# Split products for the rows' scales, a last output tile in two halves, and two rests in the second transform stage

## The chip, the core and the metric

The kernel runs on one core of one Trainium2 chip. The metric is the device time of one execution in microseconds. A core has five engines with a queue each: TensorE (PE; its weight loads are shown as PEld), VectorE (DVE), ScalarE (ACT), GpSimd (POOL) and SyncE (SP), which here only issues transfers. An engine works off its queue in order; a transfer (DMA) is issued from a queue and lands later.

## The reference

Two branches share a layer norm of q (here x); everything is fp32, S = 2048 rows, D = 576 channels, DFF = 4608.

```python
k_shift = sum(k_pad[:, t:t+S, :] * shift_k[:, ks-1-t] for t in range(4))
kv = k_shift * v
y = irfft(rfft(kv padded to 2S) * rfft(ssm_k padded to 2S))[:S] + kv * ssm_D     # per channel
...
xn = layernorm(x)
out = x + xn * y + relu(xn @ w1) @ w2
```

## The kernel before

**The FFN branch is the frame.** Tokens lie in 16 tiles of 128 rows, in two halves of 8; a half has two blocks b of 4 tiles (512 tokens). DFF is cut into 18 chunks of 256, so there are 36 "quads" g (18 for each half). A quad makes the hidden values of both blocks, `psh = w1 . x`, and the second product `pso = hidden . w2` of the quad before is made between its pieces, tile by tile. fp32 precision comes from fp32r products of split operands: each value is a rounded part (`hh`, `x[:, 0]`) plus a rest (`ll`, `x[:, 1]`), three products for one. From the fourth quad on (`PLAIN = 3`) seven products of sums replace eight. The order on PE in such a quad is: product 00, units 0 and 1, product 01, rest hl, unit 2, product s2, unit 3, product s1, unit 4, product s3, rest hl, product s4, units 5 and 6, rest hl of the second block, unit 7, product 11, rest hl. A "unit" is the 12 products of one token tile with w2 (`mm2`); DVE then adds the tile into `acc` (L752). Two results are put together on DVE (L686 `u2`, L693 `p5`), and ACT writes the negative of one PSUM bank into another (L688), which PE waits for before it adds the third `rest hl` of the quad: `y` is read by L688 and then written on by PE.

```python
nc.vector.tensor_tensor(u2, x, u2, OP.add)             # L686
x = bank(g, 0, "4")
nc.scalar.activation(x, y, AF.Copy, scale=-1.0)        # L688
hidden(g, 0, 1, u2); unit(5); unit(6)
rest(y, g, b1, 1)                                      # PE's next write of y
```

**The convolution runs in the gaps.** The generator `conv`/`stages` writes a long convolution by DFTs as a stream of steps. `tick` gives it turns: each piece of FFN work adds its cost to a clock, and steps are drawn from the stream as long as the stream's own count is not ahead. A step may yield a cost, `"wide"` (the next step needs a PSUM slot of a unit), or a negative number: a set rest, for so much FFN cost no step is drawn, and the count restarts at 0. `PAUSE` is 16000; a product of 512 columns costs 512.

**The second stage** (L987 to L1098) multiplies spectra. There are 18 rounds n. `product_of(n)` makes the spectrum of the input on PE (psf, two banks), the filter's spectrum of round n+1 (psg, a borrowed slot; ACT copies it out at L1024, SP shuffles its partitions by four DMAs at L1029), then four multiplications on DVE (L1051), which need the psf banks and the shuffled filter; four DMAs (L1056) shuffle the product. `join(n)` (L1063, DVE) needs those. `way_back(n)` does the inverse of two joined rounds. `first_spectrum` stands ahead of round 0. The output stage follows (groups of two token tiles: PE at L1157, DVE gates L1129 and adds L1137, z loaded by SP at L1114).

**The start.** The first three quads use rows that are centred but not yet scaled. The scales 1/std are spread along the free axis by a product: `diagonal` puts them on the diagonal of 128x128 blocks, `scales` multiplies by `ones` (L327), and ACT copies `row` out.

**Order.** A tracking layer sets waits between engines, and a scheduler with its own time model sets the order on each queue from the written order and `tc.issue_after`.

Of the kernel before, what the change touches and what calls it, by code (L numbers as in the profile page):

```python
# [10 lines left out]
F32 = mybir.dt.float32  # L11
F32R = mybir.dt.float32r
AF = mybir.ActivationFunctionType
OP = mybir.AluOpType
# [3 lines left out]
P = 128  # L18
# [5 lines left out]
NH = D // 2  # L24
# [6 lines left out]
BT = T // NB  # L31
# [17 lines left out]
PAUSE = 16000  # L49
# [11 lines left out]
W_FB, W_FS, W_FK, W_FX, W_FMK, W_FMX, W_FMB, W_FO = 2.8, 4.1, 2.5, 1.75, 4.0, 3.6, 2.9, 3.9  # L61
# [38 lines left out]
def h3_ffn_kernel(ctx: ExitStack, tc, x, k, v, shift_k, ssm_k, ssm_D, w1, w2, fwd, inv, mid, out):  # L100
    nc = tc.nc
    x = x[0].rearrange("(p u t) d -> u p t d", u=U, t=T)
    k = k[0].rearrange("(p u t) d -> u p t d", u=U, t=T)
    v = v[0].rearrange("(p u t) d -> u p t d", u=U, t=T)
    out = out[0].rearrange("(p u t) d -> u p t d", u=U, t=T)

    const = ctx.enter_context(tc.tile_pool(name="const", bufs=1))
# [8 lines left out]
    ident = const.tile([P, P], F32, name="ident")  # L116
    make_identity(nc, ident)
    mv = const.tile([P, T, 2], F32, name="mv")
    rstd = const.tile([P, T], F32, name="rstd")
# [20 lines left out]
    def fft_psum():  # L140
        return ps_f.tile([P, 512], F32, tag="f", name="psf")
# [9 lines left out]
    def two(t):  # L151

        return t.rearrange("p (h n) -> p h n", h=2)


    acc = {}

    def halves(u):

        return slice(u * A1, (u + 1) * A1), slice((1 - u) * A1, (2 - u) * A1)  # L160

    def move(tile_, rows, t, store=False, queues=(nc.sync, nc.sync)):
        for u in range(U):
            a, b = tile_[halves(u)[0]], rows[u, :, t]
            queues[u].dma_start(*((b, a) if store else (a, b)))
# [3 lines left out]
    def load_acc(t, **queues):  # L169
        pair = xp.tile([P, 2, D], F32, tag=f"acc{t % HT}", name=f"acc{t}")  # L170
        move(pair, x, slice(t, t + 2), **queues)
        pairs[t] = pair
        acc[t], acc[t + 1] = pair[:, 0, :], pair[:, 1, :]
# [7 lines left out]
    def inv_std(t0, n):  # L181

        q = xp.tile([P, 3, 2 * BT], F32, tag="q", name=f"q{t0}", bufs=2)[:, :, :n]
        va, h0, qu = q[:, 0, :], q[:, 1, :], q[:, 2, :]
        nc.vector.tensor_scalar(va, mv[:, t0:t0 + n, 1], EPS, None, op0=OP.add)
        nc.scalar.activation(h0, va, AF.Sqrt, scale=0.25)
        nc.vector.reciprocal(qu, h0)
        nc.vector.tensor_tensor(qu, va, qu, OP.mult)
        nc.vector.scalar_tensor_tensor(qu, qu, 0.25, h0, op0=OP.mult, op1=OP.add)
        return nc.vector.reciprocal(rstd[:, t0:t0 + n], qu)  # L190
# [6 lines left out]
    done = {}  # L197
# [116 lines left out]

    def diagonal(pool, b):
        diag = pool.tile([P, 2, D], F32, tag="xn", name=f"diag{b}", bufs=4)
        diag = diag[:, 0, :BT * P].rearrange("p (i n) -> p i n", i=BT)
        for i in range(BT):
            nc.vector.tensor_scalar(diag[:, i, :], ident, rstd[:, b * BT + i:b * BT + i + 1],
                                    None, op0=OP.mult)  # L320
        return diag

    def scales(pool, b, diag):

        ps = fft_psum()
        with tc.issue_after(done["pe"].ins):
            done["pe"] = nc.tensor.matmul(ps, ones, diag.rearrange("p i n -> p (i n)"),  # L327
                                          start=True, stop=True)
        row[b] = pool.tile([P, 512], F32, tag=f"row{b}", name=f"row{b}")
        nc.scalar.activation(row[b], ps, AF.Copy)  # L330

# [234 lines left out]
    def matmuls(ps, seq, start):  # L566


        for n, (a, m) in enumerate(seq):
            with tc.issue_after(done["pe"].ins) if "pe" in done and not n else nullcontext():  # L570
                last = nc.tensor.matmul(ps, a, m, start=start and n == 0, stop=n == len(seq) - 1,  # L571
                                        skip_group_check=True)
        done["pe"] = last
# [134 lines left out]
    def token(g, b, i):  # L708
        return (g // NQ) * HT + b * BT + i
# [16 lines left out]
    def mm2(g, b, i):  # L726
        t = token(g, b, i)
        end = g == QUADS - 1
        if end:
            while t not in added:  # L730
                next(stream)
        cols = slice(i * P, (i + 1) * P)
        ps, slot["closed"] = open_ps.pop((g, t))
        unwritten.discard(slot["closed"])
        slot["units"] += 1
        for h in range(2):
            dc = slice(h * NH, (h + 1) * NH)
            seq = []
            for f in range(FT):
                hh, ll = hid[g, b, f]  # L740
                for a, m in ((hh, 0), (hh, 1), (ll, 0)):
                    seq.append((a[:, cols], w2s[g, f][:, m, dc]))
            matmuls(ps[:, h, :NH], seq, t not in seeded)
        if t in seeded:
            done["act"] = nc.scalar.activation(two(acc[t]), ps[:, :, :NH], AF.Copy)
            seeded.remove(t)
        elif g < PLAIN:
            done["acc"] = nc.vector.scalar_tensor_tensor(two(acc[t]), ps[:, :, :NH],
                                                         rstd[:, t:t + 1], two(acc[t]),
                                                         op0=OP.mult, op1=OP.add)  # L750
        else:
            done["acc"] = nc.vector.tensor_tensor(two(acc[t]), ps[:, :, :NH], two(acc[t]), OP.add)  # L752
        tick(W_UNIT, False)
        if g == NQ - 1 and t % 2:
            nc.sync.dma_start(fin[t // 2], pairs[t - 1])
            load_acc(t - 1 + HT)
        if end:
            if b == 1 and i >= BT - 2:
                move(acc[t], out, t, store=True, queues=(nc.sync, nc.scalar))
            elif t % 2:  # L760
                move(pairs[t - 1], out, slice(t - 1, t + 1), store=True)
# [39 lines left out]
    def stages(view, views):  # L801
# [280 lines left out]
            load(zx, n, "x")  # L1082
        yield -PAUSE
        first_spectrum()
        yield W_FMK
        for n in range(NCH // 2 + 1):
            if n in pairs_n:
                yield "wide"
            if n:
                join(n - 1)  # L1090
            if n in pairs_n:
                product_of(n)
            yield W_FMK / 2 + W_FMX
            if n and n % 2 == 0:
                yield "wide"
                way_back(n - 2)
            if n:
                yield W_FMK / 2 + W_FMB  # L1098
# [112 lines left out]
    load_acc(BT + 2)  # L1211
    for j in range(FT):
        load_w2(0, j)
    ones = const.tile([P, P], F32, name="ones")
    nc.vector.memset(ones, 1.0)
    table = const.tile([P, 1], F32, name="table")
    nc.vector.memset(table, 1.0)
    nc.scalar.activation(table, table, AF.Sqrt)
# [8 lines left out]
    with tc.tile_pool(name="fa", bufs=1) as fa:  # L1227
        block_xT(fa, 0, ("00", "01"), (None, None), block_rows(fa, 0))
        xn = block_rows(fa, 1)
        classical(0, 0, 0, 1)  # L1230
        classical(0, 0, 1, 2)
        block_xT(fa, 1, ("10", "11"), ("s4", None), xn)
        load_w1(1)
        with tc.issue_after(done["low"].ins):
            inv_std(0, 2 * BT)
        with tc.issue_after(done["centred"].ins):
            for j in range(FT):
                split_w2(0, j)
                load_w2(1, j)
        classical(0, 1, 0, 0)  # L1240
        split_a(1)
        classical(0, 1, 1, 0)
        split_r(1)
        split_b(1)
        split_d(1)
        load_w1(2)
        diag = {b: diagonal(fa, b) for b in (1, 0)}

        def unit(g, b, i, upto):
            open_unit(g, b, i)  # L1250
            mm2(g, b, i)
            post(1, upto)

        for g in range(1, PLAIN):
            now = "00" if g < PLAIN - 1 else "10"
            for f in range(FT):
                for i in range(2):
                    unit(g - 1, 0, 2 * f + i, "00")
                if g == 1:
                    scales(fa, 1 - f, diag[1 - f])  # L1260
                if g == f == 1:
                    posts["at"] = second_half_of_start(fa)
                classical(g, 0, f, 0, 3, now if f else "00")
            for j in range(FT):
                split_w2(g, j)
                load_w2(g + 1, j)
            for i in range(BT):
                unit(g - 1, 1, i, now)
            classical(g, 1, 0, 0, 3, now)
            split_a(g + 1)  # L1270
            if g + 1 == PLAIN:
                sums(g + 1)
            split_r(g + 1)
            classical(g, 1, 1, 0, 3, None if g == PLAIN - 1 else now)
            split_b(g + 1)
            split_d(g + 1)
            load_w1(g + 2)
        quad(PLAIN, [(PLAIN - 1, b, i) for b in range(2) for i in range(BT)])
        post(99)
# [36 lines left out]
```

## Time and profile before

| what | value |
|---|---|
| median of 3 runs | 1026.66 us (1026.35 to 1027.32) |
| profiled execution, its own time | 1028.02 us |
| its span, first to last instruction | 1026.2 us |
| PE busy / DVE / ACT / POOL | 1011.8 / 709.2 / 429.7 / 486.8 us |
| mean granted TensorE clock | 0.998 |

Rows of the timeline read: start, duration, engine (a q behind its name is its queue, issuing), line, operation, out<-in, engine tile if any, shape, and in brackets how long the engine was idle just before and what ended it. Rows that follow each other on an engine and are alike are merged (x4). Rows of the waits read: engine, line, what it waited for: total, times, longest. Rows of the windows: each engine's busy time with its instructions, then the granted clock, the share of the DMA engines and GB/s.

### The profile page before, as it was taken

The page shows a single profiled execution, that of the slowest core. Times are in us where ns is not written, and L with a number is a line of the kernel's source. Part 1 is how long each engine was busy: PE and PEld are TensorE (multiplying, and loading weights), DVE is VectorE, ACT ScalarE, POOL GpSimd, SP SyncE. Part 2 cuts the span into 40 slices and gives each one's busy share as a digit, 9 for nine tenths or more (in the row PEclk, how much of TensorE's full clock was granted, in tenths as well). Part 3 has the DMA queues.
Part 4 walks back from the last instruction along what each step waited for, and adds up shares of the span by engine and source line. Part 5 has one row for each costly group of instructions (what it writes and reads, how often), then busy time and mean ns, then how long its engine had stood idle before and what let it go on. Part 6 is the DMA issues. An engine that isn't in the chain of part 4 may idle for free.

```text
span 1026.2 us, 17380 instructions
## 1 busy us (share of the span) xinstructions
PE 1011.8 (99%) x6506; PEld 845.9 (82%) x6506; DVE 709.2 (69%) x1075; ACT 429.7 (42%) x761; POOL 486.8 (47%) x532
## 2 busy tenths in 40 slices
PE   9999999999999999999999999989999999999997
PEld 5898999998988889888878889867767777788777
DVE  6787677776465567779787889456656676656765
ACT  7244334443344444444434444444535355332220
POOL 4335446659544557555545455414423344344450
PEclk9999999999999999999999999999999999999999
DMA  7114467558245565369943433677778887857784
GB/s 177 48 44 117 116 173 168 181 175 200 73 134 174 179 196 146 112 208 370 277 139 125 137 97 115 205 222 222 228 227 245 236 264 238 225 189 238 207 256 116
DMA packets 92249, 184.70 MB, mean 180 GB/s; under 512 B 32082, under 2 KB 44500, under 8 KB 91268
## 3 DMA queue, kind: packets, MB, share of 16 engines
q1 hardware_dynamic: 73588, 123.47, 39.8%
q0 software_dynamic: 18256, 59.22, 20.0%
q10 hardware_dynamic: 320, 0.88, 0.3%
q8 instruction: 51, 0.84, 0.3%
q14 instruction: 34, 0.28, 0.1%
HBM read 119.04 MB, written 45.61 MB: 160 GB/s over the span
## 4 chain that ended last, share of the span: by engine, by line
PE 87%; DVE 4%; POOL 2%; DMA 2%; issue 2%; ACT 1%; SPq 1%; DVEq 0%; POOLq 0%; ACTq 0%
PE pso L571 40%; PE psh L571 34%; PE psf L765 5%; PE psg L765 4%; PE psh_c L571 3%; DMA area<-area 1%; POOL area L812 1%; PE psw L1223 1%; DMA r<-in_w 1%; DVE area L944 1%; DVE area L1051 1%; DVE area L945 0%; SPq L1029 0%; DVE sums L527 0%; DVE x L295 0%
## 5 line engine op out<-in xcount | busy, mean ns | idle before, releaser
L571 PE MATMUL pso<-w,hh 128*128 128x288 f32 x2304 | 468.4, 297 | 0.0
L571 PEld LDWEIGHTS pso<-w,hh 128*128 128x128 f32 x2304 | 378.6, 188 | 34.8 <-issue 15.6
L571 PE MATMUL pso<-w,ll 128*128 128x288 f32 x1152 | 340.0, 295 | 0.0
L752 DVE TENSOR_TENSOR acc<-pso,acc 128x576 f32<-128x576 f32 x243 | 183.0, 754 | 157.4 <-PE pso L571 157.1
L571 PEld LDWEIGHTS pso<-w,ll 128*128 128x128 f32 x1152 | 216.8, 188 | 0.0
L515 POOL TENSOR_TENSOR wb<-sums,wb 128x512 fp32r<-128x512 f32 x33 | 51.2, 1552 | 236.1 <-ACT wb L514 208.5
L515 POOL TENSOR_TENSOR w<-r,w 128x576 fp32r<-128x576 f32 x72 | 107.8, 1505 | 106.9 <-ACT w L514 105.8
L571 PE MATMUL psh<-x,wa 128*128 128x512 f32 x396 | 102.9, 395 | 0.5 <-POOL wa L515 0.3
L571 PE MATMUL psh<-xs,wb 128*128 128x512 f32 x396 | 102.0, 393 | 0.0
L571 PE MATMUL psh<-hl,wr 128*128 128x512 f32 x264 | 85.9, 407 | 6.3 <-ACT psh L688 6.3
L571 PEld LDWEIGHTS psh<-x,wa 128*128 128x128 f32 x396 | 72.3, 188 | 16.1 <-POOL wa L515 0.8
L571 PEld LDWEIGHTS psh<-xs,wb 128*128 128x128 f32 x396 | 70.8, 188 | 11.4
L515 POOL TENSOR_TENSOR wa<-r,wa 128x512 fp32r<-128x512 f32 x36 | 53.7, 1490 | 52.8 <-ACT wa L514 52.8
L595 DVE SCALAR_TENSOR_TENSOR ll<-psh,hh 128x512 fp32r<-128x512 f32 x66 | 45.2, 685 | 40.9 <-ACT hh L593 40.7
L688 ACT ACTIVATE psh<-psh 128x512 f32<-128x512 f32 x33 | 19.2, 582 | 128.2 <-DVE u L686 128.2
L571 PEld LDWEIGHTS psh<-hl,wr 128*128 128x128 f32 x264 | 46.0, 188 | 27.1 <-issue 13.2
L765 PE MATMUL psf<-area 64*64 64x512 f32 (+10 forms) x592 | 61.1, 473 | 0.0
L593 ACT ACTIVATE hh<-psh 128x512 fp32r<-128x512 f32 x66 | 39.4, 597 | 49.7 <-PE psh L571 49.0
L765 PE MATMUL psg<-area 64*64 64x512 f32 (+10 forms) x568 | 55.3, 453 | 0.0
L593 ACT ACTIVATE hh<-p 128x512 fp32r<-128x512 f32 x33 | 20.9, 632 | 79.1 <-DVE p L693 43.2
L1024 ACT ACTIVATE area<-psg 128x1024 f32<-128x1024 f32 x34 | 33.2, 1025 | 48.7 <-PE psg L765 48.1
L1051 DVE TENSOR_TENSOR area<-psf,area 128x512 f32<-128x512 f32 x72 | 44.7, 681 | 9.4 <-DMA area<-area 6.7
(140 smaller groups left out, 1525.1 us busy)
## 6 DMA issues: line engine op xcount, KB each, us to landing
r<-in_w POOLq DMA_DIRECT2D x70, 288.0 KB, 3.4
area<-area SPq DMA_DIRECT2D x144, 128.0 KB, 3.8
r<-in_w POOLq DMA_DIRECT2D x35, 512.0 KB, 5.1
zk<-area SPq DMA_DIRECT2D x64, 144.0 KB, 2.3
area<-zk SPq DMA_DIRECT2D x18, 512.0 KB, 4.5
area<-zx SPq DMA_DIRECT2D x18, 512.0 KB, 3.9
zy<-area SPq DMA_DIRECT2D x18, 512.0 KB, 4.8
area<-zy SPq DMA_DIRECT2D x32, 288.0 KB, 5.4
```

The lines of the kernel that those rows point to most:

```text
L515: nc.gpsimd.tensor_tensor(w[:, 1, :n], src, w[:, 0, :n], OP.subtract)
L571: last = nc.tensor.matmul(ps, a, m, start=start and n == 0, stop=n == len(seq) - 1, skip_group_check=True)
L593: done["act"] = nc.scalar.activation(hh, ps, AF.Relu)
L595: nc.vector.scalar_tensor_tensor(ll, ps, 0.0, hh, op0=OP.max, op1=OP.subtract)
L688: nc.scalar.activation(x, y, AF.Copy, scale=-1.0)
L752: done["acc"] = nc.vector.tensor_tensor(two(acc[t]), ps[:, :, :NH], two(acc[t]), OP.add)
L765: done["pe"] = nc.tensor.matmul(ps, a, m, start=start, stop=stop, skip_group_check=True)
L812: nc.gpsimd.dma_start(kt[halves(h)[0], d:d + KD, :], src)
L944: nc.vector.tensor_tensor(e, win[t - n], sk[:, n, :], OP.mult)
L1024: nc.scalar.activation(dst, src, AF.Copy)
L1051: nc.vector.tensor_tensor(filt[c][:, k, :], banks[k], filt[c][:, k, :], OP.mult)
L1223: last = nc.tensor.matmul(idle[0], warm[:, :P], warm, start=True, stop=True)
```

## The change

Four places. (1) The scales are split into a rounded part and a rest (`inverse`, made by a copy and a subtraction on DVE), the diagonals are made by multiplications with broadcast operands, two for each block, and each of the two fp32 products becomes two fp32r products. (2) The last unit of the last quad adds and stores each 288-column half by itself, on the SP and ACT queues. (3) After the first spectrum the stream rests for 8000 instead of yielding a cost of 4.0. (4) After round 0 it rests for 12000 instead of yielding 5.6.

```diff
+        diag = diag[:, :, :BT * P].rearrange("p k (i n) -> p k i n", i=BT).bitcast(F32R)
+        for k in range(2):
+            part = inverse[:, k, b * BT:(b + 1) * BT].unsqueeze(2).to_broadcast([P, BT, P])
+            nc.vector.tensor_tensor(diag[:, k], ident.unsqueeze(1).to_broadcast([P, BT, P]),
+                                    part, OP.mult)
...
-            done["pe"] = nc.tensor.matmul(ps, ones, diag.rearrange("p i n -> p (i n)"),
-                                          start=True, stop=True)
+            for k in range(2):
+                done["pe"] = nc.tensor.matmul(ps, ones, diag[:, k].rearrange("p i n -> p (i n)"),
+                                              start=k == 0, stop=k == 1)
...
             matmuls(ps[:, h, :NH], seq, t not in seeded)
+            if end and b == 1 and i == BT - 1:
+                done["acc"] = nc.vector.tensor_tensor(acc[t][:, dc], ps[:, h, :NH], acc[t][:, dc],
+                                                      OP.add)
+                for u, queue in enumerate((nc.sync, nc.scalar)):
+                    queue.dma_start(out[u, :, t, dc], acc[t][halves(u)[0], dc])
+        if end and b == 1 and i == BT - 1:
+            return
...
         first_spectrum()
-        yield W_FMK
+        yield -PAUSE / 2
...
-            yield W_FMK / 2 + W_FMX
+            yield W_FMK / 2 + W_FMX if n else -0.75 * PAUSE
...
-    ones = const.tile([P, P], F32, name="ones")
-    nc.vector.memset(ones, 1.0)
+    ones = const.tile([P, P], F32R, name="ones")
+    nc.vector.tensor_scalar(ones, ident, 0.0, 1.0, op0=OP.mult, op1=OP.add)
+    inverse = const.tile([P, 2, 2 * BT], F32R, name="inverse")
...
             inv_std(0, 2 * BT)
+            nc.vector.tensor_copy(inverse[:, 0], rstd[:, :2 * BT])
+            nc.vector.tensor_tensor(inverse[:, 1], rstd[:, :2 * BT], inverse[:, 0], OP.subtract)
```

**Where the order changes: DVE at rounds 0 and 1.** The rows are DVE's queue in quad 25 between the adds of units 4 and 7. `sign` marks `join(0)`, `psf` the multiplications of round 1, `u2_25` is L686. Before:

```order
L752 TENSOR_TENSOR acc12_5207<-pso24_12_7027,acc12_5207 128x576
L527 TENSOR_TENSOR sums26_7128<-r1_26_6898 128x256 x2
L527 TENSOR_TENSOR sums26_7128<-sums26_7128,r1_26_6898 128x256
L1063 SCALAR_TENSOR_TENSOR area_1173<-area_1173,sign_85 128x1024
L527 TENSOR_TENSOR sums26_7128<-sums26_7128,r1_26_6898 128x256
L1051 TENSOR_TENSOR area_1173<-psf_7101,area_1173 128x512
L1051 TENSOR_TENSOR area_1173<-psf_7102,area_1173 128x512
L1051 TENSOR_TENSOR area_1173<-psf_7101,area_1173 128x512
L1051 TENSOR_TENSOR area_1173<-psf_7102,area_1173 128x512
L686 TENSOR_TENSOR u2_25_7025<-psh25_5_7041,u2_25_7025 128x512
```

And now (L686 has become L688, L1051 L1060, L1063 L1072):

```order
L529 TENSOR_TENSOR sums26_7101<-sums26_7101,r1_26_6899 128x256 x2
L688 TENSOR_TENSOR u2_25_7026<-psh25_5_7042,u2_25_7026 128x512
L761 TENSOR_TENSOR acc12_5208<-pso24_13_7081,acc12_5208 128x576
L597 SCALAR_TENSOR_TENSOR ll25_0_1_7123<-u2_25_7026,hh25_0_1_7122 128x512
L761 TENSOR_TENSOR acc14_5290<-pso24_14_7126,acc14_5290 128x576
L1072 SCALAR_TENSOR_TENSOR area_1174<-area_1174,sign_85 128x1024
L695 TENSOR_TENSOR p5_25_7076<-psh25_2_6934,p5_25_7076 128x512
L1060 TENSOR_TENSOR area_1174<-psf_7157,area_1174 128x512 x2
L1060 TENSOR_TENSOR area_1174<-psf_7158,area_1174 128x512 x2
```

`u2_25` now stands ahead of round 1's join and multiplications. On PE round 1 moves from behind product s3 of quad 25 to behind the third rest hl; round 0 keeps its place.

**DVE at rounds 7 and 8.** All later rounds shift too. PE's places in quads 25 to 29, with s1, s2, s3, x01 for the products, hl for the second rest, hl3 for the third: before, round 5 behind s2 and round 6 behind hl in quad 27, round 7 behind x01 and round 8 behind s1 in quad 28, round 9 behind product 11 of 28, round 10 behind s2 of 29; now round 5 behind s1 and 6 behind hl3 in 27, 7 behind s2 and 8 behind s3 in 28, 9 behind x01 and 10 behind s1 in 29, with the fifth way back behind hl of 29. DVE's queue in quad 28 had no round between the add of unit 4 (`pso27_12`) and `u2_28`; now it has:

```order
L761 TENSOR_TENSOR acc12_5208<-pso27_12_7971,acc12_5208 128x576
L1072 SCALAR_TENSOR_TENSOR area_1174<-area_1174,sign_85 128x1024
L529 TENSOR_TENSOR sums29_8045<-r1_29_7818 128x256 x2
L1060 TENSOR_TENSOR area_1174<-psf_8018,area_1174 128x512 x2
L529 TENSOR_TENSOR sums29_8045<-sums29_8045,r1_29_7818 128x256
L1060 TENSOR_TENSOR area_1174<-psf_8019,area_1174 128x512 x2
L529 TENSOR_TENSOR sums29_8045<-sums29_8045,r1_29_7818 128x256
L688 TENSOR_TENSOR u2_28_7969<-psh28_5_7985,u2_28_7969 128x512
```

Round 8's join and multiplications stand ahead of `u2_28`, as round 1's and round 6's stood ahead of `u2_25` and `u2_27` before.

**PE at the last unit.** The rows are PE's queue for the last tile, with the semaphores that a row waits for (DVE_49 counts DVE's instructions):

```order
L573 MATMUL pso35_15_10354<-w235_10068,hh35_1_0_10243 128x288 [waits DVE_49]
L573 MATMUL pso35_15_10354<-w235_10068,hh35_1_0_10243 128x288
L573 MATMUL pso35_15_10354<-w235_10068,ll35_1_0_10244 128x288
L573 MATMUL pso35_15_10354<-w235_10146,hh35_1_1_10212 128x288 x2
L573 MATMUL pso35_15_10354<-w235_10146,ll35_1_1_10213 128x288
L573 MATMUL pso35_15_10354<-w235_10068,hh35_1_0_10243 128x288 [waits DVE_49]
L573 MATMUL pso35_15_10354<-w235_10068,hh35_1_0_10243 128x288
```

Before, only the first of the twelve products waited; now the seventh, the first of the second half, waits for DVE as well. Its count in the built program is that of the first half's add: both halves lie in one PSUM tile.

**DVE at the scales**, behind the last `ll` of the first quad. Before, the eight `diag` rows stood ahead of the first `acc0`; now the first `acc0` stands between the copy and the subtraction:

```order
L1246 CAST inverse_127<-rstd_84 128x8
L757 SCALAR_TENSOR_TENSOR acc0_104<-pso0_0_436,rstd_84,acc0_104 128x576
L1247 TENSOR_TENSOR inverse_127<-rstd_84,inverse_127 128x8
L320 TENSOR_TENSOR diag1_430<-ident_78,inverse_127 128x512
L320 TENSOR_TENSOR diag0_433<-ident_78,inverse_127 128x512
L320 TENSOR_TENSOR diag1_430<-ident_78,inverse_127 128x512
L320 TENSOR_TENSOR diag0_433<-ident_78,inverse_127 128x512
```

Block 1's second diagonal, which the first of the two scale products needs, is DVE's sixth row from here.

More of the change, by code (lines that the diff above doesn't have):

```diff
@@ L316, in diagonal @@
         diag = pool.tile([P, 2, D], F32, tag="xn", name=f"diag{b}", bufs=4)
[L317 to L320, printed above, removed]
+        diag = diag[:, :, :BT * P].rearrange("p k (i n) -> p k i n", i=BT).bitcast(F32R)
[3 more added lines that the diff above has]
+                                    part, OP.mult)
         return diag
@@ L757, in mm2 @@
         if end:
-            if b == 1 and i >= BT - 2:
+            if b == 1 and i == BT - 2:
                 move(acc[t], out, t, store=True, queues=(nc.sync, nc.scalar))
```

## Prediction

> **What bounds the kernel.** I read the page's busy shares first, then the waits of PE, then windows of 20 us, then the timeline where the windows show PE short.
>
> ```profile
> PE 1011.8 (99%) x6506; PEld 845.9 (82%) x6506; DVE 709.2 (69%) x1075; ACT 429.7 (42%) x761; POOL 486.8 (47%) x532
> PE psh L571 <- ACT psh L688: 6.3, 3, 2.7
> 500.00:520.00 20.00, 18.89 (x117) 16.96 (x115) 17.71 (x22) 6.50 (x11) 11.13 (x11) 1.00 0.83 228
> 520.00:540.00 20.00, 19.16 (x125) 16.56 (x126) 16.12 (x22) 9.68 (x18) 9.63 (x11) 0.91 0.48 139
> 680.00:700.00 20.00, 17.31 (x107) 14.15 (x103) 13.08 (x21) 6.57 (x11) 5.70 (x7) 1.00 0.71 194
> 740.00:760.00 20.00, 18.33 (x120) 14.12 (x120) 13.07 (x22) 7.51 (x12) 4.23 (x5) 1.00 0.81 217
> ```
>
> PE is the bound. Time can come only from its few gaps, from work taken off it, or from the ends. Three waits for L688 make 6.3 us; one lies near 520, in the first stage, where the order is unchanged. The other two lie in the second stage. The first:
>
> ```profile
> 674.32 1.09 PE L765 MATMUL psf<-area 64*64 64x512 f32 x8
> 677.51 2.48 DVE L1051 TENSOR_TENSOR area<-psf,area 128x512 f32<-128x512 f32 x4 [3.71 <-DMA area<-area]
> 679.37 1.80 PE L765 MATMUL psf<-area 64*64 64x512 f32 x8
> 681.93 2.45 SPq L1029 DMA_DIRECT2D area<-area  x4
> 683.73 1.29 DVE L1063 SCALAR_TENSOR_TENSOR area<-area,sign 128x1024 f32<-128x1024 f32 x1 [2.07 <-DMA area<-area]
> 686.20 2.48 DVE L1051 TENSOR_TENSOR area<-psf,area 128x512 f32<-128x512 f32 x4 [0.84 <-DMA area<-area]
> 688.60 0.68 DVE L686 TENSOR_TENSOR u<-psh,u 128x512 f32<-128x512 f32 x1
> 689.95 0.74 PE L571 MATMUL psh<-hl,wr 128*128 128x512 f32 x2 [2.69 <-ACT psh L688]
> ```
>
> Round 0 starts at 674.32, round 1 already at 679.37. Its multiplications L1051 need the filter that the L1029 transfers shuffle, queued on SP behind round 0's. They land at 686.20. DVE stands still for them, L686 is queued behind, ACT's L688 behind that, and PE misses 2.69 us. Round 1's psf also took 1.80 instead of 1.09: the banks were still being read by round 0's L1051.
>
> ```profile
> 738.13 1.09 PE L765 MATMUL psf<-area 64*64 64x512 f32 x8
> 739.39 2.47 DVE L1051 TENSOR_TENSOR area<-psf,area 128x512 f32<-128x512 f32 x4
> 746.62 1.09 PE L765 MATMUL psf<-area 64*64 64x512 f32 x8
> 748.90 1.28 DVE L1063 SCALAR_TENSOR_TENSOR area<-area,sign 128x1024 f32<-128x1024 f32 x1 [2.59 <-DMA area<-area]
> 750.93 1.29 DVE L1051 TENSOR_TENSOR area<-psf,area 128x512 f32<-128x512 f32 x2 [0.41 <-DMA area<-area]
> 753.67 0.68 DVE L686 TENSOR_TENSOR u<-psh,u 128x512 f32<-128x512 f32 x1
> 755.02 0.73 PE L571 MATMUL psh<-hl,wr 128*128 128x512 f32 x2 [1.67 <-ACT psh L688]
> ```
>
> The second is the same chain between rounds 5 and 6, 8.5 us apart. From a round's start to the next filter's landing it was 11.9 us (674.32 to 686.20) and 12.8 us (738.13 to 750.93). A third pair, rounds 7 and 8, has 11.4 us (767.16 to 778.60):
>
> ```profile
> 767.16 1.09 PE L765 MATMUL psf<-area 64*64 64x512 f32 x8
> 775.66 1.09 PE L765 MATMUL psf<-area 64*64 64x512 f32 x8
> 778.60 2.48 DVE L1051 TENSOR_TENSOR area<-psf,area 128x512 f32<-128x512 f32 x4 [1.19 <-DMA area<-area]
> ```
>
> There no PE time was lost: round 8 stood behind product s1, with unit 4, s3, hl and s4 still ahead of L686. So what decides is the distance of a round to the one before, and whether L1051 stands ahead of `u2` on DVE.
>
> **The rests.** By the order, round 1 goes behind the third rest hl, where `u2_25` and `p5_25` are ahead of its multiplications: the wait of 2.69 us goes. So do the 0.71 us of psf (1.80 - 1.09), since round 0's L1051 ends at 679.99 and round 1 now starts about 685. Late next there is the add of unit 7, behind L1051 until about 688.7; its slot is not needed again before two products and a unit have passed, over 4 us: nothing. Round 6 also goes behind the third hl: 1.67 us go. The rest of 8000 alone moves no row of PE: round 0 keeps its place, as it had to wait for a free slot anyhow.
>
> SP issues the same DMAs, each later with its round, and only loads of zk change places with shuffles. ACT's copies L1024 fall behind `hh` rows and POOL's loads of inv and stores of out behind weight splits; both queues are idle over half the span (42% and 47% above), which hides that. The last output group moves from behind s3 to behind the third hl of quad 35, some 5 us; its stores have the last eight units (8 x 1.59, half of the row 37.32 below) to land in.
>
> But all rounds shift, and one pair becomes tight. Round 8 is now behind s3, round 7 behind s2 of the same quad: between their starts lie 8.0 us, the 8.5 of rounds 5 and 6 without the two products of hl. Round 5 stood in exactly this place behind s2, with a way back ahead of it at the same distance, so I take its 12.8 us to the landing. L686 then follows 3.1 us later (750.93 to 753.67 is 2.74, plus one more of the `sums`, about 0.4, that now stands between). PE resumes 1.35 us after L686's start (753.67 to 755.02). That is 12.8 + 3.1 + 1.35 = 17.25 us after round 7's start; PE would arrive without a wait at 15.22 (755.02 - 1.67 - 738.13; the same work). A new wait of 2.0 us. With a landing after 11.4 us it is 0.6; one that never holds DVE makes it 0. The ends are 0 and 2.4. I take 1.9, by the row of the same place.
>
> Round 10, 8.5 us behind round 9, is the second tight pair; its L1051 end before `u2_29` is due, but the fifth way back, a round, a unit, s3 and hl later (5.5 us), needs its psf banks. With a landing after 11.4 us the first bank is free at 4.8 (2.9 and three of the four L1051), with 12.8 at 6.2: 0 to 0.7 us; I take 0, since the row of this pair (7 and 8 above) is 11.4. Sum of the rests: -2.69 - 0.71 - 1.67 + 1.9 = -3.2 us.
>
> **The scales.**
>
> ```profile
> 29.56 0.17 DVE L189 SCALAR_TENSOR_TENSOR q<-q 128x8 f32<-128x8 f32 x1
> 30.77 3.03 DVE L319 TENSOR_SCALAR diag<-ident,rstd 128x128 f32<-128x128 f32 x8
> 41.27 1.89 DVE L340 TENSOR_TENSOR xf<-xf,row 128x512 f32<-128x512 f32 x3
> 46.93 0.98 DVE L340 TENSOR_TENSOR xf<-xf,row 128x512 f32<-128x512 f32 x1
> 32.97 1.12 PE L327 MATMUL psf<-diag,ones 128*128 128x512 f32 x2 [0.29 <-DVE diag L319]
> 34.10 3.22 PE psh_c L571 x14
> 37.32 3.18 PE pso L571 x24
> 40.50 0.86 PE psf L327 x2
> ```
>
> On the chain (the last three rows) the second fp32 product costs 0.86 us; an fp32r product of the same shape costs 0.23 (3.22/14), two of them 0.46. The second scales save 0.40. The first wait for DVE: from 30.77 a copy (0.17 as the 128x8 row), the add that now stands between (0.76 as in the rows of the last tile below; unit 0 ends one unit, 1.59, before PE's idle time ahead of 32.97, at 31.1), a subtraction (0.17) and three multiplications of 0.63 (1.89/3) give 34.0, plus a product of 0.23 and its start: the next product starts at 34.3 instead of 34.10. Worse by 0.2; by 1.3 if the multiplications take 0.98, as one did beside POOL, and better by 0.4 if DVE is early. Together -0.2 (-0.8 to +0.9). `ones` from `ident` lies in DVE's idle time before the first row arrives.
>
> **The last tile.**
>
> ```profile
> 1019.48 0.76 DVE L752 TENSOR_TENSOR acc<-pso,acc 128x576 f32<-128x576 f32 x1 [0.84 <-PE pso L571]
> 1021.08 0.76 DVE L752 TENSOR_TENSOR acc<-pso,acc 128x576 f32<-128x576 f32 x1 [0.83 <-PE pso L571]
> L1129 DVE SCALAR_TENSOR_TENSOR area<-area,mv,psf x16: 500/513/515, 930.2 to 998.2; 128x288 f32<-128x288 f32 x16
> out<-acc SPq DMA_DIRECT2D x2, 144.0 KB, 3.2
> ```
>
> Alone, halving would end the last add after 0.5 (L1129's 128x288) instead of 0.76: -0.26. But PE's second half now waits for the first half's add. PE ends just before 1021.08, and its first half 0.8 earlier, at 1020.25; the add runs to about 1020.8; PE starts again, ends at 1021.65, the add at 1022.2 instead of 1021.84: +0.3. The smaller store may land sooner; its bounds are 0 and -0.5, and I take 0. [...]
>
> **The sum.** -3.2 - 0.2 + 0.3 = -3.1 us: the profiled execution's 1028.02 would be 1024.9. The median is 1026.66, 1.36 lower; the half-clock piece at 520 (0.09 of 20 us, 1.8 us lost) may account for that, if it does not occur in each execution. On the median, -3.1 gives 1023.6.
>
> **The rivals.** *No new wait* (chance 0.22): round 7's transfers are as quick as the quickest landings, and round 8 costs 0. Against it: the row of the same place. Gain 5.0: 1021.6.
>
> *Half clock* (0.22). Behind the wait near 520, of 1.95 us by the window rows (1.11 + 0.84), the granted clock fell to 0.91 over 20 us; behind 2.69 us at 687 it stayed 1.00. A new wait of 2 us in quad 28 can meet the same and lose another 1.8: 1025.4, within 0.2% of before. [...]
>
> *Slower* (0.07): the output stage.
>
> ```profile
> 940.17 1.19 PE L765 MATMUL psf<-area 128*64 128x288 f32 x8
> 941.19 1.14 PE L765 MATMUL psg<-area 128*64 128x288 f32 x8
> 941.38 2.49 SPq L1114 DMA_DIRECT2D area<-zy  x4
> DMA to landing us min/median/max: 3.3/5.4/8.1
> ```
>
> A group takes PE about 2.1 us (940.17 to 942.33), and the z of the next but one is issued up to 3.7 us after its start. By the order the first group is now behind the third hl of quad 33 and the third behind hl of 34: two groups, three units (7, 0, 1), products 11, 00, 01 (1.38 each) and two rests apart, 14.0 us. PE waits once a landing takes over 10.3 us, and each microsecond more is one on PE: at 13.4 the forecast's gain is gone, at 15.5 the kernel is slower by 0.2%. Against it: the slowest of 32 landings took 8.1.
>
> *The rests only move the wait* (0.04), by L1051 at its new places holding back L688 or the unit slots all the same: 1026.5.
>
> **Numbers.** The forecast, 0.45, has 1022.6 to 1025.0 as its own range. A difference of 0.2% (2.05 us) is about what a measurement can tell here: faster means under 1024.6. Faster: 0.9 of the forecast's 0.45, the 0.22 of no new wait: 0.62. Same: the rest, with the half clock: 0.31. Slower 0.07. The range runs from no new wait with the scales at their best (0.6 better than taken), 1021.0, to the half clock with round 8 and the second tight pair at their upper ends (+0.5 and +0.7), 1026.5.
>
> **What would show it.** In the trace after: no wait of PE for the L688 row (now L690) near 687 and 753; instead one of about 2 us in quad 28, near 780; round 1's psf at 1.09; the scale rows at 0.46 on the chain, with the first product behind them at 34.3; the last add about 0.3 later than PE's end would give. I am wrong if quad 28 shows no wait, if a clock below 1.00 appears in the second stage, or if a `psf` row of the output stage waits for z.

## The result, and the profile after

The changed kernel is slower: 1033.49 us in the median of 5 executions (1030.98 to 1035.41) against 1026.66 before, a ratio of 1.0063 (95% interval 1.0043 to 1.0083), some 6.5 us. The forecast was 1023.6, with slower at 7%. The profiled execution of after is the quickest of its five, with a span of 1029.2 us against 1026.2, so the two traces hold only 3.0 us of the difference.

The waits of TensorE in the profile after (engine and line, what it waited for, total, times, longest):

```profile
PE psh L573 <- ACT psh L690: 4.9, 3, 2.4
PE psh L573 <- ACT wa L516: 1.4, 1, 1.4
PE psf L329 <- DVE diag L320: 1.4, 2, 0.7
PE psh L573 <- POOL wa L517: 1.1, 1, 1.1
PE pso L573 <- DVE acc L747: 0.6, 1, 0.6
```

L690 is the old L688. It still holds PE three times. The windows of 20 us say where; the first number behind the length is PE's busy time, the 1.00 or 0.91 near the end the granted clock:

```profile
240.00:260.00 20.00, 17.46 (x103) 15.19 (x102) 10.33 (x14) 6.01 (x12) 16.14 (x18) 1.00 1.02 185
520.00:540.00 20.00, 19.31 (x140) 16.64 (x139) 16.40 (x24) 8.83 (x17) 10.19 (x11) 1.00 0.58 170
680.00:700.00 20.00, 20.00 (x129) 15.28 (x128) 16.89 (x26) 7.10 (x12) 6.14 (x7) 1.00 0.83 221
740.00:760.00 20.00, 20.00 (x127) 16.63 (x124) 15.62 (x24) 8.35 (x13) 6.00 (x7) 1.00 0.86 244
780.00:800.00 20.00, 18.02 (x115) 13.03 (x114) 12.36 (x20) 9.18 (x16) 5.81 (x7) 1.00 0.70 196
900.00:920.00 20.00, 17.56 (x98) 14.26 (x97) 9.08 (x15) 5.71 (x11) 5.11 (x7) 0.91 0.37 113
```

The windows at 680 and 740, short of PE before, are now full: both old waits are gone. The one at 780 is the new wait of quad 28 that was forecast, between rounds 7 and 8 (the columns: start, duration, engine, line, operation, and in brackets the idle time ahead and what ended it):

```profile
765.90 1.09 PE L774 MATMUL psf<-area 64*64 64x512 f32 x8
773.94 1.09 PE L774 MATMUL psf<-area 64*64 64x512 f32 x8
778.49 1.29 DVE L1060 TENSOR_TENSOR area<-psf,area 128x512 f32<-128x512 f32 x2 [0.15 <-DMA area<-area]
781.56 0.68 DVE L688 TENSOR_TENSOR u<-psh,u 128x512 f32<-128x512 f32 x1
782.91 0.73 PE L573 MATMUL psh<-hl,wr 128*128 128x512 f32 x2 [1.80 <-ACT psh L690]
```

Two windows were not forecast: 240 to 260, in the first stage where the order of instructions is the same, and 900 to 920. At 240 PE waits for weights:

```profile
255.38 0.63 ACT L516 ACTIVATE wa<-r 128x512 fp32r<-128x512 f32 x1 [1.70 <-DMA r<-in_w]
256.06 0.73 PE L573 MATMUL psh<-x,wa 128*128 128x512 f32 x2 [1.40 <-ACT wa L516]
256.13 1.74 POOL L517 TENSOR_TENSOR wa<-r,wa 128x512 fp32r<-128x512 f32 x1
257.92 1.20 PE L573 MATMUL psh<-x,wa 128*128 128x512 f32 x4 [1.14 <-POOL wa L517]
```

The load of raw weights r landed at 255.4. Before, ACT could start the same split at 252.02, and PE lost 0.35 us:

```profile
252.02 0.62 ACT L514 ACTIVATE wa<-r 128x512 fp32r<-128x512 f32 x1
254.24 1.20 PE L571 MATMUL psh<-x,wa 128*128 128x512 f32 x4 [0.35 <-POOL wa L515]
```

And in quad 32, around 911:

```profile
896.72 1.09 PE L774 MATMUL psf<-area 64*64 64x512 f32 x8
897.98 2.47 DVE L1060 TENSOR_TENSOR area<-psf,area 128x512 f32<-128x512 f32 x4
899.88 2.46 SPq L1065 DMA_DIRECT2D area<-area  x4
908.52 1.28 DVE L1072 SCALAR_TENSOR_TENSOR area<-area,sign 128x1024 f32<-128x1024 f32 x1 [4.16 <-DMA area<-area]
910.06 0.68 DVE L688 TENSOR_TENSOR u<-psh,u 128x512 f32<-128x512 f32 x1
911.41 0.92 PE L573 MATMUL psh<-hl,wr 128*128 128x512 f32 x2 [2.44 <-ACT psh L690]
```

Round 17, the last, starts at 896.72. Its shuffled product lands 11.8 us later; `join(17)` (L1072) waits for it on DVE, the add L688 is queued behind, L690 behind that, and PE misses 2.44 us. The granted clock is half from 911.78 to 915.19, for 3.41 us. PE wanted the add at 907.6 (911.41 less the wait of 2.44 and the 1.35 from the add to PE), 10.9 us after the round's start. Before, there were 12.6 us between the two, and the product was there in time:

```profile
895.45 1.09 PE L765 MATMUL psf<-area 64*64 64x512 f32 x8
905.43 1.27 DVE L1063 SCALAR_TENSOR_TENSOR area<-area,sign 128x1024 f32<-128x1024 f32 x1
908.06 0.69 DVE L686 TENSOR_TENSOR u<-psh,u 128x512 f32<-128x512 f32 x1 [0.34 <-PE psh L571]
```

### The profile page after: what moved, and what is told of

Same layout as the page of the kernel before. It is cut to its first block, busy times and chain, and to the rows that moved or that the text cites. A ratio compares the mean times of both kernels' runs of the same rounds, so it can differ in the third digit from the quotient of the medians.

```text
span 1029.2 us, 17387 instructions
## 1 busy us (share of the span) xinstructions
PE 1012.8 (98%) x6506; PEld 845.5 (82%) x6506; DVE 710.3 (69%) x1074; ACT 429.6 (42%) x761; POOL 487.9 (47%) x532
## 4 chain that ended last, share of the span: by engine, by line
PE 86%; DMA 4%; DVE 4%; issue 2%; POOL 2%; ACT 1%; SPq 1%; DVEq 0%; POOLq 0%; ACTq 0%
PE pso L573 40%; PE psh L573 33%; PE psf L774 5%; PE psg L774 4%; PE psh_c L573 3%; DMA area<-area 1%; DMA area<-in_ssm_k 1%; PE psw L1233 1%; DMA out<-area 1%; POOL area L821 1%; DMA r<-in_w 1%; SPq L1065 1%; DVE area L1060 0%; DVE x L295 0%; DVE area L954 0%
## 5 line engine op out<-in xcount | busy, mean ns | idle before, releaser
L573 PEld LDWEIGHTS psh<-xs,wb 128*128 128x128 f32 x396 | 70.8, 188 | 11.4
L690 ACT ACTIVATE psh<-psh 128x512 f32<-128x512 f32 x33 | 19.2, 582 | 123.1 <-DVE u L688 123.1
L573 PE MATMUL psh<-x,wc 128*128 128x512 f32 x198 | 51.3, 394 | 0.0
```

## The experiments

All medians and ratios below stand against the kernel before, run on the same chip in turns with them.

**The parts one by one.** The kernel before once more, and then with one part of the change each: the scales (all hunks of `diagonal`, `scales`, `ones`, `inverse`), the halves (`mm2`), the rests (the two `yield` lines).

The kernel before again:

> The kernel before, unchanged, profiled and timed once more, to see what one execution differs from another. Theory (the shift of +2.5 us near 254 us of the profile after, and of -2.8 us near 520, belong to the execution and not to the change): ratio 1.000 within 0.002, and the waits of 2.69 and 1.67 us in the second stage are there again, while the waits in the first stage (near 254: 0.35 before, 2.54 after; near 520: 1.95 before, 0.69 after) and the moment at which the clock doubles at the start (5.6 and 7.2 us) differ from the first profile. Rival (a kernel's first stage repeats itself): all three as in the first profile within 0.3 us.

Only the scales:

> Only the split scales. Theory (the terms read from the two traces: +0.9 at the first scales, -0.5 at the second): +0.4 us, 1027.1, ratio 1.0004 (0.999 to 1.002); PE waits twice for the diagonals, 1.4 us in all. Rival (the later start of the first stage moves weight loads against the filter's loads on GpSimd's queue, and the +2.5 us near 254 come from that): +2.5 to +4, about 1030, with a wait of over 2 us there.

Only the halves:

> Only the last output tile by halves. Theory (PE's second half waits 0.55 us for the first half's add; the last add is 0.3 us shorter, and from PE's end to the end of the span the profile has 4.4 us after against 5.5 before): -0.7 us, 1026.0, ratio 0.9993. The prediction's term was +0.3: 1027.0, 1.0003. Rival (the stores of halves queue behind the seven stores before them on the SyncE queue): +1 or more.

Only the rests:

> Only the two rests. Theory (both waits go, -5.8 us, and four new ones take their place: quad 28 +2.4, quad 32 +2.6, quad 35 +1.1; then a window of half clock behind some of these): 1027 to 1031, ratio 1.000 to 1.004, with waits of PE for L688 in quads 28 and 32 and a clock under 1.00 behind at least one of them in most executions. Rival 1, the prediction's sum: 1023.5, 0.997, quad 32 undisturbed. Rival 2 (the rests are not the cause of the loss; scales and halves are): ratio under 0.999.

| kernel | median us | ratio (95%) |
|---|---|---|
| before again | 1026.99 | 1.0004 (0.9990 to 1.0017) |
| only the scales | 1031.02 | 1.0040 (1.0026 to 1.0054) |
| only the halves | 1025.99 | 0.9989 (0.9978 to 1.0000) |
| only both rests | 1028.82 | 1.0019 (1.0006 to 1.0032) |

The kernel before repeats its second-stage waits (2.69 and 1.78 us), and its wait near 254 was 1.00 instead of 0.35, so the theory that the 2.5 us there belong to the execution seemed possible. The scales alone refute it: they cost 4.1 us, ten times the theory's 0.4, with 2.3 us of waits near 254. The rival's cost and the spot in time fit; whether its reason does, the next runs show. The halves alone came out as their theory had it, -0.9 us, with an interval that ends at no change. The rests alone lose, as the theory said, with three waits for L688:

```profile
PE psh L571 <- ACT psh L688: 5.9, 3, 3.5
```

These are 1.95 us in quad 28, 3.54 in quad 32 and the rest, about 0.4, in the first stage. The theory's further wait in quad 35 is not in the trace.

**Why the scales cost 4 us: the place of a tile.** With the scales alone the order of instructions is the same on ACT, POOL and SP, and on PE and DVE but for the scales' own rows. What else differs is the allocation. `inverse` takes 64 bytes of each partition, so everything allocated behind it lies 64 bytes further on: the area of the convolution starts at byte 174528 of a partition instead of 174464. The filter is loaded to its start, `area<-in_ssm_k`, by GpSimd ahead of weights r on the same queue. So the next kernel moves the place and nothing else, and a second one moves it by another 64 bytes:

```diff
+    const.tile([P, 16], F32, name="spare")
     table = const.tile([P, 1], F32, name="table")
```

In the kernel before:

> The kernel before with one unused tile of 64 bytes per partition allocated ahead of `table`: no instruction is changed, added or moved, but all tiles behind it, the convolution's area among them, lie 64 bytes further on, as they do behind the tile `inverse` of the split scales. Theory (the place decides: it makes the filter's loads slow, whose 4096-byte packets took 365 ns in the mean with the split scales and 291 to 303 without): 1029.5 to 1031, ratio 1.003 (1.002 to 1.004), waits of PE for the weights wa of over 2 us in all near 254, and packets over 350 ns there. Rival (the later start of the first stage by 0.4 us decides, by the moment at which loads meet): 1.000 within 0.0015, packets under 310 ns, as in the kernel before.

With the split scales:

> The split scales alone, with the same unused tile of 64 bytes: `inverse` and it together move the area by 128 bytes. Theory (the place): the wait near 254 is under 1.2 us, the packets are back at about 300 ns, and what is left is the scales' own +0.4: 1027.3, ratio 1.0004 (0.9990 to 1.0018). Rival (the later start): 1031, 1.004, as without the tile.

The unused tile alone made the kernel before slower by 1.0044 (1.0029 to 1.0059), 1030.99 us, at the upper end of its theory's range. With the scales, a second 64 bytes brought 1.0040 down to 1.0012 (1.0002 to 1.0023), 1027.94. The theory of the place held and the rival of the later start fell. The filter's loads by row of the DMA issues (count, size of each, median us from issue to landing) and by their spread, in this order: before, after, the spare tile alone, the scales with the spare tile:

```profile
area<-in_ssm_k POOLq DMA_DIRECT2D x16, 288.0 KB, 6.9
DMA to landing us min/median/max: 4.6/6.9/9.2
```

```profile
area<-in_ssm_k POOLq DMA_DIRECT2D x16, 288.0 KB, 8.0
DMA to landing us min/median/max: 5.3/8.0/13.1
```

```profile
area<-in_ssm_k POOLq DMA_DIRECT2D x16, 288.0 KB, 7.9
DMA to landing us min/median/max: 5.1/7.9/12.6
```

```profile
area<-in_ssm_k POOLq DMA_DIRECT2D x16, 288.0 KB, 6.9
DMA to landing us min/median/max: 4.5/6.9/9.6
```

And PE's waits of the kernel with the spare tile alone, which has not one instruction more than the kernel before:

```profile
PE psh L571 <- POOL wa L515: 1.1, 1, 1.1
PE psh L571 <- ACT wa L514: 1.0, 1, 1.0
```

The packets of 4096 bytes on GpSimd's queue between 215 and 262 us took 363 to 371 ns in the mean in the four traces with the area at 174528 (scales, after, spare tile, after with one rest) and 289 to 303 in the ten with it at 174464 or 174592. So the loads are slower, the weights that share the queue land later, and PE waits for `wa` twice. The weights r moved by the same 64 bytes, but that is not what slows them: their loads issued before 215 or after 262 us landed after 4.25 us in the median before and 4.27 with the spare tile. The two waits are 2.2 us, where the two traces of the kernel before have 0.35 and 1.00; where the rest of the 3.8 us lies is open. Of the three places, 174464 and 174592 are multiples of 128 bytes and 174528 is not; why the packets take longer there, no run here shows.

**The rests: which one loses.** Rounds stand at known places of PE's order. The table has the distance in us from the start of the last round whose result DVE needs ahead of the add `u2` to the third rest hl of that quad, from the traces, with PE's waits for L688 taken out (in quad 25 of before, 0.7 of the 12.9 is round 1's slow psf).

| quad | 25 | 26 | 27 | 28 | 29 | 30 | 31 | 32 |
|---|---|---|---|---|---|---|---|---|
| before | **12.9** | 20.6 | **15.2** | 18.5 | 27.0 | 20.5 | 27.0 | 15.5 |
| both rests | none | 20.6 | 26.5 | **15.2** | 20.6 | 20.6 | 20.5 | **12.3** |
| first rest alone | none | 20.5 | 27.0 | 18.5 | 27.0 | 20.6 | 27.0 | 15.5 |

In these three traces the waits of over 1 us for L688 in the second stage stand at the bold places and nowhere else. The first expectation below has shorter distances (10.2, 13.3, 12.0, 15.6): they were counted in the program, where a transform is one instruction, while the trace has two for each. So its clear gap between 13.3 and 15.6 is not there. 15.2 us waits and 15.5 does not, but different work stands behind them: in quads 27 and 28 the next round's four multiplications (2.5 us) follow on DVE ahead of the add, in quad 32 only `join(17)` (1.3 us).

On all queues the second rest alone gives the same order as both, so the first does nothing beside it. The first alone gives another order, without the bold places. That was the forecast of the next two:

```diff
         first_spectrum()
-        yield W_FMK
+        yield -PAUSE / 2
```

> Only the first rest, 8000 behind the first spectrum; round 0's turn stays at 5.6. By the order of instructions the rest of 12000 alone gives the same order on PE and DVE as both rests, while this one gives another. Theory (a wait for L688 comes where the round whose shuffled filter or product DVE needs ahead of it started under about 15 us before, counted in PE's undisturbed time: 10.2 and 13.3 where the kernel before waits 2.69 and 1.67; 13.3 and 12.0 where the kernel with both rests waits): the least distance here is 15.6, so no wait for L688 behind 600 us, -4.4 to -5.5 us, 1022, ratio 0.9953 (0.994 to 0.997). Rival (a rest only moves the waits elsewhere, as both rests did): 1.000 to 1.002, with a wait of over 1 us in another quad of the second stage.

> The first rest and the last output tile by halves, without the second rest and without the split scales. Theory (the two terms add): -4.9 and -0.9, 1021.1, ratio 0.9944 (0.993 to 0.996). Rival (the first rest does nothing): 0.999.

The first rest alone: 1020.33 us, 0.9947 (0.9931 to 0.9963); its twelve executions lie between 1018.72 and 1026.60. With the halves: 1021.03, 0.9950 (0.9937 to 0.9963), not to be told from it. Of all waits for L688 this is left with the first rest alone, and it lies near 520:

```profile
PE psh L571 <- ACT psh L688: 0.3, 1, 0.3
```

With the halves, the trace has one wait of 0.82 us for L688 in quad 26, at the long distance: there the shuffled filter of round 3 landed 16.0 us after round 2's start (693.46 to 709.51), where the landings in the prediction took 11.4 to 12.8. So a long distance makes a wait unlikely and does not rule it out.

**Undoing the two causes in the changed kernel**: the spare tile of 64 bytes, the second rest taken back (`yield W_FMK / 2 + W_FMX` as before), and both.

> The changed kernel, with the unused tile of 64 bytes that brings the area back to a multiple of 128 bytes. Theory (two causes, place and second rest, add): the place's +3.2 to +3.8 us go, 1029.5 to 1030.5, ratio 1.003 (1.0015 to 1.0045); wait near 254 under 1.2 us, waits in quads 28 and 32 as in the changed kernel. Rival (something else of the changed kernel costs the rest of its 6.8 us): over 1032.

> The changed kernel without its second rest, the first rest kept. Theory: the first rest's -6 us, and the place's +3.5 and the scales' +0.5 stay: 1024 to 1025, ratio 0.9975 (0.996 to 0.999); no wait for L690 of over 1 us behind 600 us. Rival (the split scales shift the rounds too, so that the waits come back): 1.000 or more.

> The changed kernel with both: the unused tile and no second rest. Theory: the kernel with the first rest and halves, and the scales' own +0.4 to +0.9: 1021.5, ratio 0.995 (0.9935 to 0.9965). Rival (a cause is missing): 0.997 or more.

| changed kernel | median us | ratio to before (95%) |
|---|---|---|
| as it is | 1033.49 | 1.0063 (1.0043 to 1.0083) |
| with the spare tile | 1030.23 | 1.0024 (1.0005 to 1.0044) |
| without the second rest | 1024.04 | 0.9973 (0.9963 to 0.9982) |
| both | 1022.31 | 0.9955 (0.9943 to 0.9967) |

All three fell where the theory had them (the last 0.8 us above its value, inside its range). With the spare tile quad 32 alone cost 4.15 us in the trace, and 6.83 us at half clock; without the second rest one trace has a wait of PE of 2.40 us for ACT near 467 that no other shows; its cause is open. The two causes carry the result: with the place set right and without the second rest the change gains 0.45%, about 4.6 us.

**The last tile.** The second half of the last output tile got a PSUM tile of its own, so that PE need not wait for the first half's add (on the kernel with the first rest and halves):

```diff
+            last = end and b == 1 and i == BT - 1
+            half = fft_psum()[:, :NH] if last and h else ps[:, h, :NH]
-            matmuls(ps[:, h, :NH], seq, t not in seeded)
+            matmuls(half, seq, t not in seeded)
```

> The kernel before with the first rest and the last output tile by halves, the second half of the last tile in a PSUM tile of its own. Theory (PE's 0.55 us there is a wait for the tile that both halves share): PE waits for no add at the end, and the last add ends 0.55 us sooner than with the shared tile, measured from the start of the last unit; time -0.5 against that kernel: 1020.5, ratio 0.9942 (0.993 to 0.9955). Rival (the wait is for the add's read of the PSUM, or the end is set by the stores alone): no change, 0.995.

The rows of the end, first with the shared tile (the profile after), then with two:

```profile
1023.51 0.46 DVE L747 TENSOR_TENSOR acc<-pso,acc 128x288 f32<-128x288 f32 x1
1024.02 0.53 PE L573 MATMUL pso<-w,hh 128*128 128x288 f32 x2 [0.55 <-DVE acc L747]
1024.06 2.01 SPq L750 DMA_DIRECT2D out<-acc  x2
1025.12 0.46 DVE L747 TENSOR_TENSOR acc<-pso,acc 128x288 f32<-128x288 f32 x1 [1.16 <-PE pso L573]
```

```profile
1013.16 0.46 DVE L747 TENSOR_TENSOR acc<-pso,acc 128x288 f32<-128x288 f32 x1
1013.71 1.92 SPq L749 DMA_DIRECT2D out<-acc  x2
1013.96 0.46 DVE L747 TENSOR_TENSOR acc<-psf,acc 128x288 f32<-128x288 f32 x1 [0.35 <-PE psf L571]
```

The wait is gone, so it was the shared tile. But the end of the span did not move: from the start of the last unit the last add ends after 2.25 us with two tiles and 3.06 with one (1012.17 to 1014.42; 1012.30 to 1015.36 in the kernel with first rest and halves), and the span ends after 6.66 and 6.68. The time is 1021.26, 0.9946 (0.9934 to 0.9958): the rival that the stores alone set the end fits better. The stores hardly left earlier: on SP the last one is issued from 2.57 to 3.47 us after the start of the last unit with two tiles and from 3.09 to 3.55 with one, so its issue begins 0.52 sooner, takes twice as long and ends 0.08 sooner. Why it takes longer is open.

## Why the prediction was wrong

- **The two old waits go: right.** The windows at 680 and 740 are full.
- **A new wait of 2.0 us in quad 28: right,** 1.80 us in the trace (1.95 with the rests alone), by the mechanism given: from round 7's start to the multiplications of round 8 it took 12.6 us (12.8 taken), to PE's start 17.0 (17.25), and without a wait it would have been 15.2 (15.22). Round 1's psf is back at 1.09, and the second tight pair cost nothing, as taken.
- **"But all rounds shift, and one pair becomes tight": the step that failed for the rests.** I searched the pairs of rounds, where DVE waits for the *filter* of the round before. `join` waits for the round's *product* in the same way, and round 17's join stands alone ahead of quad 32's add. With the rests its distance fell from 15.5 to 12.3 us, and PE lost 2.44 us (3.54 with the rests alone). That term was absent. With it the sum of the rests is -0.8 instead of -3.2, ahead of any loss of clock. The rests alone measured +1.9: in their trace quad 32 cost 1.1 us more than in the profile after, and both new waits were followed by half clock.
- **"The rest of 8000 alone moves no row of PE": wrong.** Alone it moves round 1 and others behind it and gains 0.5%; no kernel here is clearly faster. It does nothing only where the second rest follows it. I took the two rests as one term and so never saw that the second spoils what the first brings.
- **The scales: the step that failed worst is that no term was given to `inverse` as an allocation.** Its 64 bytes cost 3 to 4 us (1031.02 with the scales against 1027.94 with the spare tile; 1030.99 against 1027.21 for the tile alone). No rival held it, and the range could not.
- **The scales' own cost was too low.** I took 0.17 us for the copy and as much for the subtraction, from a row of eight columns; in the profile after they took 0.51 and 0.74:

```profile
31.59 0.51 DVE L1246 CAST inverse<-rstd 128x8 fp32r<-128x8 f32 x1
32.74 0.74 DVE L1247 TENSOR_TENSOR inverse<-rstd,inverse 128x8 fp32r<-128x8 f32 x1
33.40 2.48 DVE L320 TENSOR_TENSOR diag<-ident,inverse 128x512 fp32r<-128x512 f32 x4
34.13 0.50 PE L329 MATMUL psf<-diag,ones 128*128 128x512 f32 x1 [0.64 <-DVE diag L320]
35.34 0.50 PE L329 MATMUL psf<-diag,ones 128*128 128x512 f32 x1 [0.71 <-DVE diag L320]
```

  In two other traces the subtraction took 0.15 and the four multiplications 3.03, so the lost half microsecond lies between the two and is not shown to be the subtraction's. DVE also makes the rounded parts of both blocks' diagonals before the rests of either (four multiplications, 2.48 us), so PE waits a second time, 0.71 us, between its two products. With the scales alone, PE's units stand 0.9 us later behind the first scales than in the kernel before, and 0.5 later behind the second. The second scales save the 0.4 that was forecast; the first were mis-sized, +0.9 for +0.2. Together that is +0.5 where I had -0.2. The experiment gives 0.12% (0.02 to 0.23).
- **The last tile: the wait right, the end wrong.** PE waits 0.55 us as worked out. But from the start of the last unit the span ends 0.33 us sooner (6.68 with halves, 7.01 with the first rest alone), since from the last add to the end it takes 3.6 us instead of 4.4 (1025.58 to 1029.2; 1021.84 to 1026.2). I took 0 for the smaller store, with -0.5 as the bound; that part got 0.8 shorter. The experiment's -0.9 agrees in sign only: its interval reaches 0, and with the first rest the halves gained nothing that could be told.
- **The half clock, a rival at 0.22, came true beside the rest,** in the profile after behind quad 32 and not behind quad 28. The mean granted clock was 0.9950 in the 5 executions after and 0.9975 in 35 before: of the span that is 5.2 and 2.5 us, a difference of 2.7 of the 6.5. (A part of each lies in the last microseconds, where PE has no work: in the profile after, the clock is half from 1027.8 to the end at 1029.2.) So a wait can cost a second time; with the first rest alone the clock was 0.9988.
- **The rival that said slower (0.07) is not what happened.** In the profile after no psf row of the output stage waits for z. That the kernel is slower has other causes, so the direction of that rival was right by luck.

Added from the experiments: place +3.1, scales' own +1.2, both rests +1.9, halves -0.9, together +5.3 against the 4.4 to 8.5 of the interval. Each of these terms is uncertain by about a microsecond.

## What to carry to other kernels

A new constant tile, here 64 bytes of each partition, moves everything allocated behind it: write the start of each large buffer before and after, and if it has moved, try the change also with a spare tile that moves it on. (Three places were run here: 64 bytes further on the filter's loads landed after 7.9 and 8.0 us in the median, at the old place and 128 bytes further on after 6.9; which other places cost time is not known.) When work is moved in a stream, list for every engine queue *all* instructions that wait for a transfer (here the joins as well as the filters) and the distance from their source to the next instruction on the critical engine behind them; a distance that gets shorter then shows in the order, without a run. Count it in the instructions of the trace, and only compare places with the same work behind them. And take apart a change with two knobs on one stream: one of them may be the whole gain and the other its loss.

## What the runs showed of the hardware

- **Half clock came in pieces of 3.413 us, in or just behind some of PE's waits of 1.8 to 4.2 us.** In the 14 traces, each piece of half clock between the start and the end is 3.413 us long (two are 6.827), and each begins during a wait of PE of 1.8 to 4.2 us or within 1.4 us of its end. Of 21 waits of 1.5 us or more, 11 had such a piece; of shorter waits, none. The stretches of full clock between are whole multiples of 3.413 us too (151, 265 and 200 of them up to the first piece in before, after and before again). With each trace divided into stretches of 3.413 us from the moment at which its clock doubled at the start, half clock followed on each of the 11 stretches at full clock in which PE was idle for 1.81 us or more, and on none of those with 1.71 or less. In the two long pieces the wait ran on into the stretch of half clock. Some of them:

| kernel | wait of PE us, its end | most idle time in one stretch | half clock from |
|---|---|---|---|
| before | 1.95, 520.85 | 1.95 | 521.0 |
| before | 2.69, 689.95 | 1.71 | none |
| before again | 2.69, 687.00 | 2.33 | 688.1 |
| only the halves | 1.81, 751.81 | 1.81 | 753.2 |
| only both rests | 1.95, 780.27 | 1.95 | 781.4 |
| after | 1.80, 782.91 | 1.02 | none |
| after | 2.44, 911.41 | 2.44 | 911.8 |

  Half clock followed on a wait of 2.69 us in one execution (before again) and not in another (before), where 0.98 us of it lay in one stretch and 1.71 in the next. These are counts of this program's traces; what sets the clock, no run here shows.
- **The start varies by up to 3.3 us in when the clock doubles** (3.9 to 7.2 us from the start of the span in these traces). The warm-up products start every 0.43 us until then and every 0.215 behind it, and the first products of the program behind them start 7.96 to 8.93 us after the span's start.
- **64 bytes of offset made loads of 288 KB take 14% longer to land** (6.9 and 7.9 us in the median, 9.2 and 12.6 at the most, before and with the spare tile alone), with the same instructions, sizes and queue.
